# Mirror transposes spread one to a half block pair, and even batches' logits half a pair later

## The chip, the cores and the metric

The kernel runs on one core of one Trainium2 chip. The metric is device time in microseconds (us) of one launch; lower is better. The engines are PE (TensorE), DVE (VectorE), ACT (ScalarE), POOL (GpSimd) and SP (SyncE, which here only issues DMAs). Each engine takes its own instructions in the order in which they were written.

## The reference, cut to what matters

Attention without a softmax, gated by `u`, then a mixture of experts over every token. Eight sequences of 2816 tokens, width 256, query width 64:

```python
scores = (1 / S) * z @ z.T              # one z for queries and keys: scores are symmetric
attn   = np.maximum(scores, 0.0) ** 2
x      = (u * (attn @ v)).reshape(N, D) # N = 22528, D = 256

y      = relu(x @ w1_dense) @ w2_dense
e      = argmax(x @ w_gate, axis=1)     # 8 experts
y     += gate * relu(x @ w1[e]) @ w2[e] # one expert for each token, gate = its softmax weight
```

## The kernel before, in words

**Blocks, pairs, groups.** Each sequence (here called an attention batch) is 22 blocks of 128 tokens. `av` (line 525) works on a pair of blocks: in two passes `p` over the 22 key blocks `x` it adds up `attn @ v` for both in one pair of PSUM banks, 88 small matmuls (line 552). Between the passes and at the end `tick` runs, once for each block. Pairs belong to groups: each attention batch has a group of two blocks and then five of four, 48 groups in all. A group's relu-squared scores lie in a tile `A`, of which three buffers exist (line 74), so group n+3 is written where group n lay. The tile framework makes the first write into a reused buffer wait for all readers of its former content, DMAs included.

**Scores and their mirror.** `scores` (line 368) puts products of `z` into a PSUM pair; `relu` (line 390) has ACT or DVE copy them out (lines 398, 400) and then ACT, DVE or POOL square them into `A` (lines 411, 413). Since scores are symmetric, a group n need not compute those key blocks that are the rows of group n-2: `far_steps` (line 436) yields up to four steps, each of which issues one DMA transpose from the tile of group a = n-2 into the tile of group n (line 446) on SP's queue. Steps wait in the list `turning`, are put there when group a's first pair begins, and are taken from it within `av` at fixed `x` (line 559), if the planner holds their source ready.

**The planner.** The order on PE, ACT, DVE and SP is fixed at build time. Python code keeps a clock `now`, which each matmul advances, and a time at which each engine comes free; `offer` and `run` hand work to the engine that is free first, `fill` puts the scores of later groups between the matmuls of `av`, and `key_at` says from when a key block of a group may be read. In its first pass over a group `av` reads the key blocks in the order of `key_at` (line 543). None of these times is enforced on the chip: there an instruction waits only for its place in its queue and for its data.

**Gate and transposed rows.** When a pair is done, `gate_x` (line 575) has DVE multiply it by `u` into `pays` and SP transpose it into `xT` (line 581); SP also loads `ut`, the rows of `u`, two pairs ahead into three buffers (line 146).

**Routing.** Blocks are routed in batches `q` of 11 (line 42), unaligned with the pairs. `routing(q)` is queued at a tick, and at the next `fill` with a free PSUM pair `logits` (line 599) multiplies the batch's 11 `xT` blocks by `w_gate` (line 607). DVE and ACT then find each token's expert and place, and POOL scatters the rows to the experts' regions in DRAM. Since 11 is odd, a batch with even q ends on the first block of a pair and a batch with odd q on the second. After attention the experts' part runs from the scattered rows.

Of the kernel before, what the change touches and what calls it, by code (L numbers as in the profile page):

```python
# [19 lines left out]
def kernel(  # L20
# [23 lines left out]
    starts = [sum(sizes[:q]) for q in range(len(sizes) + 1)]  # L44
# [39 lines left out]
    def banks(x, name, shape=(P, 2, 4 * P), dt=F32):  # L84

        return ps.tile(list(shape), dt, name=name, tag=f"b{x}")
# [46 lines left out]
    now = [0.0]  # L133
# [7 lines left out]
    def load_u(g, gate=False):  # L141
        ut = aw.tile([P, 2, D], F32, name="ut", bufs=3)
        if gate:
            nc.vector.memset(ut[:, 0, 0:1], 0.0)
        b, i = divmod(g, nK)
        nc.sync.dma_start(out=ut[:], in_=uf[:, b, i:i + 2, :])
        ut_of[g] = ut[:]
# [134 lines left out]
    def offer(ready, rank, ways, then=None):  # L282
        count[0] += 1
        todo.append((rank, count[0], ready, ways, then))
# [44 lines left out]
    def until(cond):  # L329

        while cond() is None:
            pick = best()
            assert pick is not None
            now[0] = max(now[0], pick[0][0])
            give(pick)
        now[0] = max(now[0], cond())
        run(now[0])

    def pe(t):
        now[0] += t  # L340
        run(now[0])


    left, far, key_at = {}, {}, {}
# [7 lines left out]
    def open_group(n):  # L352
        if n not in A:
            A[n] = aA.tile([P, nK, 4 * P], BF, name="A", tag="A")
# [6 lines left out]
    def take_pair():  # L361
        return pairs.pop(0)[1]

    def give_pair(t, x):
        pairs.append((t, x))
        pairs.sort()
# [64 lines left out]
    def can_turn(n, m):  # L431
        _, i0, w = groups[n]
        ts = [key_at.get((m, k)) for k in range(i0, i0 + w)]
        return None if None in ts else max(ts)

    def far_steps(a):

        n = a + 2
        if n >= len(groups) or far[n] != [a]:
            return []  # L440
        (b, i0, w), (_, j0, wj) = groups[n], groups[a]

        def step(i):
            assert n - 1 in A
            open_group(n)
            nc.sync.dma_start_transpose(out=A[n][:, j0:j0 + wj, i * P:(i + 1) * P],
                                        in_=A[a][:, i0 + i, :wj * P])
            if i == w - 1:
                for j in range(wj):
                    key_at[n, j0 + j] = now[0] + 10.0  # L450

        return [(a, lambda i=i: step(i)) for i in range(w)]

# [2 lines left out]
    def fill(n, force=False):  # L456

        if jobs and jobs[0][0] <= now[0] and room(1):
            jobs.pop(0)[1]()
            return True  # L460
        m = ahead(n)
        busy = sum(1 for op in todo if op[0] in (1, 4))
        if m is not None and room(1) and busy <= (4 if n < 2 else 2):
            scores(m, left[m].pop(0))
            return True
        return False
# [7 lines left out]
    def v_at(n, k):  # L474

        return 3.3 + 2.6 * (4 * k // nK) if n == 0 else 0.0

    def need(n, k):

        while max(key_at.get((n, k), 9e9), v_at(n, k)) > now[0]:  # L480
            if fill(n):
                continue
            pick = best()
            ts = [t for t, _ in pairs if t > now[0]]
            ts += [max(key_at[n, k], v_at(n, k))] if (n, k) in key_at else []
            assert pick is not None or ts
            if pick is not None and (not ts or pick[0][0] <= min(ts)):
                now[0] = max(now[0], pick[0][0])
                give(pick)
            else:  # L490
                now[0] = min(ts)
        run(now[0])

    turning = []
# [8 lines left out]
    def swap_rows(n):  # L503

        keep[0] = 0
        if ahead(n) is None:
            until(lambda: pairs[0][0] if pairs else None)
            x = take_pair()
            touch(x)
            touch(x)  # L510
            give_pair(now[0] + 0.1, x)
            return
        until(lambda: pairs[1][0] if len(pairs) > 1 else None)
        x = take_pair()
        touch(x)
        m = ahead(n)
        scores(m, left[m].pop(0))
        m = ahead(n)
        if m is None:
            touch(x)  # L520
            give_pair(now[0] + 0.1, x)
        else:
            scores(m, left[m].pop(0), x)

    def av(n, i, between):
        b, i0, w = groups[n]
        if i == i0:
            turning.extend(far_steps(n))
        keep[0] = 0
        if n == 0 and i == i0:  # L530

            fill(n)
            need(n, 0)
        until(lambda: pairs[0][0] if pairs else None)
        ox = take_pair()
        o = banks(ox, "o")
        for p in range(2):
            rest = list(range(nK))
            for x in range(nK):
                k = rest[0]  # L540
                if i == i0 and p == 0:

                    k = min(rest, key=lambda k: (max(key_at.get((n, k), 9e9), v_at(n, k)), k))
                    need(n, k)
                rest.remove(k)
                if n == 0 and i == i0 and p == 0 and x in (12, 14, 16):
                    load_u(2 * (x - 12) // 2, gate=True)
                for h in range(2):
                    r = slice(h * dq, (h + 1) * dq)
                    j = p ^ h  # L550
                    c = (i + j - i0) * P
                    nc.tensor.matmul(out=o[:, j, 0:D], lhsT=A[n][r, k, c:c + P],  # L552
                                     rhs=v_of[b][r, k, :], start=(p == 0 and x == 0),
                                     stop=(p == 1 and x == nK - 1))
                pe(0.1092)
                keep[0] = 2 - p if x >= nK - 12 else 0
                if x % 2 == 1 and x < nK - 1:
                    fill(n)
                if x % 7 == 3 and turning:
                    t = can_turn(turning[0][0] + 2, turning[0][0])  # L560
                    if t is not None and t <= now[0] and turning[0][0] + 1 in A:
                        turning.pop(0)[1]()
            if p == 0:
                swap_rows(n)
                between()

        def done(t):
            give_pair(t + 0.1, ox)

        g = b * nK + i  # L570
        offer(now[0] + 0.2, 0, {"dve": (0.63, lambda eng: gate_x(g, o))}, done)
        keep[0] = 0


    def gate_x(g, o):
        g0 = g % (2 * G)
        x = pays[:, g0:g0 + 2, 0:D]
        assert g + 1 < 2 * G or (g - 2 * G in placed and g + 1 - 2 * G in placed)
        nc.vector.tensor_mul(x, o[:, :, 0:D], ut_of.pop(g))  # L579
        xT = aw.tile([P, 5, P], BF, name="xT", bufs=8)  # L580
        nc.sync.dma_start_transpose(
            out=xT[:], in_=pays[:, g0:g0 + 2, :].rearrange("p n r -> p (n r)")[:, 0:5 * P])
        for j in range(2):
            xT_of[g + j] = xT[:, 3 * j:3 * j + 2, :]
# [397 lines left out]
    def at(tick, fn):  # L982
        later.setdefault(tick, []).append(fn)
# [10 lines left out]
    for b in range(B):  # L994
        t = b * nK
# [38 lines left out]
    def routing(q):  # L1034
        def first():
            bank_of[q] = take_pair()
            logits(q)
            now[0] += 0.6
            offer(now[0] + 0.2, 0, {"dve": (1.3, lambda eng: route_a(q))}, middle)

        def middle(t):
            give_pair(t, bank_of[q])
            jobs.append((t + 2.5, second))

        def second():
            bank_of[q] = take_pair()
            route_pre(q)
            now[0] += 0.25
            chain(now[0] + 0.2, route_b(q), last)

        def last(t):
            give_pair(t, bank_of[q])
            routed.append(q)
            waiting.extend(range(starts[q], starts[q + 1]))

        jobs.append((now[0], first))
# [11 lines left out]
    LAG = 5  # L1068
    for q in range(nQ - 2):
        t = starts[q + 1] - 1 + LAG  # L1070
        at(t, lambda q=q: routing(q))
    for n, q in enumerate((nQ - 2, nQ - 1)):
        at(nB + 2 * n, lambda q=q: late_routing(q))
        at(nB + 2 * n + 1, lambda q=q: late_places(q))
# [36 lines left out]
    for s in range(NT - MAYBE + 2):  # L1111
# [4 lines left out]
        if s % 3 == 1 and waiting:  # L1116
# [5 lines left out]
    n = nc.values_load(used[0:1, 0:1], min_val=0, max_val=NH,  # L1122
                       skip_runtime_bounds_check_because="made by the table")
# [34 lines left out]
```

## Time and profile before

| | us |
|---|---|
| median of 3 runs | 885.77 (883.65 to 889.91) |
| the profiled execution | 887.47 |
| its span, first to last instruction | 885.8 |
| PE busy | 864.5 |
| ACT busy | 738.6 |
| DVE busy | 701.2 |
| POOL busy | 485.2 |
| mirror transposes issued (`A<-A`) | 128 |
| `xT` transposes issued | 88 |

Durations come from the profiled execution. Busy time is the time in which an engine has an instruction of its own at work; issuing a DMA and waiting are not counted. A timeline row gives start, duration, engine, source line, operation, the tile written and read, the count, and in brackets the idle time of the engine before it with what ended that. `SPq` rows are the DMA issues of SP's queue: their duration is that of the issue, and the data lands later. Attention takes about the first 560 us, the experts' part the rest.

### The profile page before, as it was taken

Reading aid. Unit: us, or ns where it says so; the run is one execution under the profiler, and the core shown is the slowest. Engines: PE = TensorE matmul, PEld = TensorE weight load, DVE = VectorE, ACT = ScalarE, POOL = GpSimd, SP = SyncE. Lnnn points to the kernel's source line nnn. Section 1 sums busy time; section 2 is a strip of 40 time slices with the busy share of each in tenths; the row PEclk is TensorE's granted clock in tenths of the full one; section 3 lists DMA queues with packets and bytes.
Section 4 is the critical chain, followed back from the end, with each engine's and each line's share of the span. In section 5 each row is a group of like instructions: output and inputs, shape, how many; then the busy total and the mean of one; then the engine's idle time right before and its main releaser. Section 6 shows DMA issues by size and latency. Waiting matters only on the chain.

```text
span 885.8 us, 30592 instructions
## 1 busy us (share of the span) xinstructions
PE 864.5 (98%) x12257; PEld 759.7 (86%) x12257; DVE 701.2 (79%) x1320; ACT 738.6 (83%) x913; POOL 485.2 (55%) x532
## 2 busy tenths in 40 slices
PE   8999999999998999999999999999999999999996
PEld 5788888898886888888888888888888888889996
DVE  7999999998996999999998997656665445546664
ACT  7999998998996998998998997477777777777774
POOL 8203343434533534434434544488888888887665
PEclk9999999999999999999999999999999999999998
DMA  6795997998898899899899896555565555544333
GB/s 148 148 174 117 146 185 145 172 174 170 153 165 168 154 181 190 127 197 198 131 196 172 151 159 112 103 133 128 129 132 122 117 120 121 123 113 110 97 100 82
DMA packets 257871, 127.64 MB, mean 144 GB/s; under 512 B 225470, under 2 KB 232894, under 8 KB 257728
## 3 DMA queue, kind: packets, MB, share of 16 engines
q1 hardware_dynamic: 230112, 70.24, 47.6%
q0 software_dynamic: 27616, 55.44, 29.2%
q8 instruction: 96, 1.57, 0.8%
q14 instruction: 47, 0.39, 0.2%
HBM read 61.54 MB, written 37.16 MB: 111 GB/s over the span
## 4 chain that ended last, share of the span: by engine, by line
PE 73%; DVE 7%; issue 6%; POOL 6%; DMA 4%; ACT 3%; SPq 0%; POOLq 0%; DVEq 0%; ACTq 0%
PE o L552 37%; PE h_ps L909 14%; PE yy L917 13%; PE s L383 8%; POOL out_dram L935 5%; DMA xT<-pays 3%; DVE r L400 2%; DVE A L413 2%; ACT A L411 1%; POOL A L413 1%; PE lg L607 1%; ACT r L398 1%; DVE pays L579 1%; DMA out_dram<-ring,ix 1%; DVE zn L113 1%
## 5 line engine op out<-in xcount | busy, mean ns | idle before, releaser
L552 PE MATMUL o<-vb,A 64*128 64x256 bf16 x7744 | 493.7, 270 | 2.6 <-POOL A L413 1.8
L552 PEld LDWEIGHTS <-A 64*128 64x128 bf16 x7744 | 408.1, 94 | 53.9 <-POOL A L413 3.0
L697 POOL DMA_INDIRECT xs<-pays,pi x176 | 196.9, 1119 | 271.1 <-DVE pi L695 207.1
L398 ACT ACTIVATE r<-s 128x1024 f32<-128x1024 f32 x274 | 270.0, 1011 | 26.1 <-PE s L383 22.1
L411 ACT ACTIVATE A<-r 128x1024 bf16<-128x1024 f32 (+1 forms) x257 | 261.3, 1042 | 5.3 <-DMA A<-A 2.7
L912 ACT ACTIVATE ring<-h_ps 128x1024 bf16<-128x1024 f32 x180 | 183.9, 1023 | 89.2 <-PE h_ps L909 87.3
L413 DVE TENSOR_TENSOR A<-r 128x1024 bf16<-128x1024 f32 x167 | 201.8, 1221 | 5.8 <-DMA A<-A 4.0
L400 DVE TENSOR_SCALAR r<-s 128x1024 f32<-128x1024 f32 (+1 forms) x158 | 190.5, 1214 | 4.3 <-POOL A L413 1.8
L933 DVE SCALAR_TENSOR_TENSOR ring<-yy,me,ring 128x256 f32<-128x256 f32 x180 | 86.8, 482 | 123.0 <-ACT ring L932 86.3
L935 POOL DMA_INDIRECT out_dram<-ring,me x140 | 146.4, 1046 | 39.8 <-issue 23.5
L383 PE MATMUL s<-zT 64*128 64x512 bf16 (+1 forms) x944 | 157.9, 359 | 1.6 <-ACT zT L192 0.6
L917 PEld LDWEIGHTS <-ring 128*128 128x128 bf16 x1440 | 140.0, 98 | 16.2 <-issue 0.3
L917 PE MATMUL yy<-w2d,ring 128*128 128x256 bf16 x720 | 108.0, 273 | 0.1
L917 PE MATMUL yy<-ring 128*128 128x256 bf16 x720 | 108.0, 273 | 0.0
L909 PE MATMUL h_ps<-ring,w1d 128*128 128x256 bf16 x720 | 93.3, 273 | 0.8 <-DVE pays L579 0.8
L909 PE MATMUL h_ps<-ring 128*128 128x256 bf16 (+1 forms) x880 | 93.7, 253 | 0.0
L897 DVE COPY ring<-wall 128x2048 bf16 x110 | 80.7, 748 | 8.6 <-DVE ring L933 4.2
L909 PEld LDWEIGHTS <-ring 128*128 128x128 bf16 x880 | 74.3, 98 | 6.8
L909 PEld LDWEIGHTS <-w1d 128*128 128x128 bf16 x720 | 70.1, 98 | 9.0 <-issue 1.0
L579 DVE TENSOR_TENSOR pays<-o,ut 128x512 bf16<-128x512 f32 x88 | 60.3, 685 | 17.6 <-PE o L552 17.1
L383 PEld LDWEIGHTS <-zT 64*128 64x128 bf16 x944 | 58.0, 94 | 16.0 <-issue 3.4
L932 ACT COPY ring<-yy 128x256 f32<-128x256 f32 x180 | 66.1, 367 | 1.8 <-PE yy L917 1.8
(120 smaller groups left out, 358.0 us busy)
## 6 DMA issues: line engine op xcount, KB each, us to landing
ut<-in_u_dram SPq DMA_DIRECT2D x88, 256.0 KB
vb<-in_v_dram POOLq DMA_DIRECT2D x16, 384.0 KB
vb<-in_v_dram POOLq DMA_DIRECT2D x16, 320.0 KB
wall<-in_moe_w_dram POOLq DMA_DIRECT2D x16, 256.0 KB
xs<-pays,pi POOLq DMA_INDIRECT x176
zr<-in_z_dram POOLq DMA_DIRECT2D x7, 352.0 KB
out_dram<-ring,me POOLq DMA_INDIRECT x140
A<-A SPq DMA_TRANSPOSE x128
```

The costliest lines, as they stand in the source:

```text
L383: nc.tensor.matmul(out=s[:, h, y * c:(y + 1) * c], lhsT=zT[r, k + h, :], rhs=zT[r, i0:i0 + w, :], start=True, stop=True)
L398: nc.scalar.activation(r[:, :, :c], s[:, :, :c], AF.Relu, scale=1.0 / S)
L400: nc.vector.tensor_scalar(out=r[:, :, :c], in0=s[:, :, :c], scalar1=1.0 / S, scalar2=0.0, op0=ALU.mult, op1=ALU.max)
L411: nc.scalar.activation(a, r, AF.Square)
L413: (nc.gpsimd if eng == "pool" else nc.vector).tensor_mul(a, r, r)
L552: nc.tensor.matmul(out=o[:, j, 0:D], lhsT=A[n][r, k, c:c + P], rhs=v_of[b][r, k, :], start=(p == 0 and x == 0), stop=(p == 1 and x == nK - 1))
L697: ins = nc.gpsimd.indirect_dma_start(out=xs, out_offset=bass.IndirectOffsetOnAxis(ap=pi[:], axis=0), in_=pays[:, g % (2 * G), 0:ROW].bitca ...
L909: nc.tensor.matmul(out=h_ps[:, f, hs, :], lhsT=w1(c, f), rhs=xT[:, hs, c, :], start=(c == 0), stop=(c == 1))
L912: nc.scalar.activation(h, h_ps[:].rearrange("p f h t -> p f (h t)"), AF.Relu)
L917: nc.tensor.matmul(out=y[:, k, :], lhsT=h[:, f, j * P:(j + 1) * P], rhs=w2(f), start=(f == 0), stop=(f == 3))
L933: nc.vector.scalar_tensor_tensor(out=ys, in0=y[:, 1, :], scalar=me[:, j, 0:1], in1=yd, op0=ALU.mult, op1=ALU.add)
L935: ins = nc.gpsimd.indirect_dma_start(out=out, out_offset=bass.IndirectOffsetOnAxis(ap=ids[j], axis=0), in_=ys, in_offset=None, bounds_chec ...
```

## The change

Two edits, and a number that goes with the first:

- a mirror step is taken at `x == 3` of the first pass and at `x == 10` of the second, where it was taken at x = 3, 10 and 17 of both. So a pair hands out two steps, one in each half, where it handed out a group's four one after the other;
- the key blocks that a group gets by mirror are held readable 6 planner units after the last step, where it was 10;
- the logits of a batch with even q are queued one tick later (`starts[q + 1]` is odd there), in the middle of a pair instead of at its end; those with odd q stay.

```diff
             if i == w - 1:
                 for j in range(wj):
-                    key_at[n, j0 + j] = now[0] + 10.0
+                    key_at[n, j0 + j] = now[0] + 6.0
...
                 if x % 2 == 1 and x < nK - 1:
                     fill(n)
-                if x % 7 == 3 and turning:
+                if x == (3, 10)[p] and turning:
                     t = can_turn(turning[0][0] + 2, turning[0][0])
                     if t is not None and t <= now[0] and turning[0][0] + 1 in A:
                         turning.pop(0)[1]()
...
     LAG = 5
     for q in range(nQ - 2):
         t = starts[q + 1] - 1 + LAG
-        at(t, lambda q=q: routing(q))
+        at(t + starts[q + 1] % 2, lambda q=q: routing(q))
```

## The prediction

> **What bounds the kernel now.** I read the page's engine table first, then the attention stage alone, then what TensorE waited for.
>
> ```profile
> PE 864.5 (98%) x12257; PEld 759.7 (86%) x12257; DVE 701.2 (79%) x1320; ACT 738.6 (83%) x913; POOL 485.2 (55%) x532
> ...
> 10.30:562.90 552.60, 542.16 (x9130) 470.77 (x9130) 511.29 (x914) 499.91 (x544) 227.58 (x225) 0.99 0.94 160
> 562.90:885.80 322.90, 315.62 (x3060) 284.38 (x3059) 182.98 (x395) 231.93 (x362) 249.66 (x288) 0.99 0.50 116
> ```
>
> The second and third rows are stretches: length, then busy time of PE, PEld, DVE, ACT, POOL, the granted clock and the DMA share. Both edits lie in the first stretch, attention. TensorE is busy 542.2 of 552.6 us there, so no more than some 10 us can be won; but DVE (511.3) and ACT (499.9) are nearly as full, and the DMA engines have a share of 0.94. A stall of DVE or ACT thus finds little slack to go into.
>
> ```profile
> PE lg L607 <- DMA xT<-pays: 6.6, 4, 4.2
> PE o L552 <- POOL A L413: 1.8, 2, 0.9
> ...
> DVE A L413 <- DMA A<-A: 4.0, 2, 3.2
> ...
> ACT A L411 <- DMA A<-A: 2.7, 1, 2.7
> ```
>
> In the table of waits (total us, times, longest) TensorE's largest is the logits' wait for the transposed rows xT, 6.6 us in four places. The two rows below decide what I forecast: squares on DVE and ACT that write a score buffer A sometimes wait for a mirror transpose that still reads the buffer's former content. So far that costs 6.7 us.
>
> ```profile
> 128.67 5.24 DMA xT<-pays
> 195.11 6.75 DMA xT<-pays
> 266.14 7.33 DMA xT<-pays
> 470.88 7.60 DMA xT<-pays
> ```
>
> The chain of waits holds the four late xT transfers: issue time, and time from issue to landing. All four belong to even batches. The worst, on the timeline:
>
> ```profile
> 257.36 0.68 DVE L579 TENSOR_TENSOR pays<-o,ut 128x512 bf16<-128x512 f32 x1
> 258.29 7.18 SPq L446 DMA_TRANSPOSE A<-A  x4
> 265.57 0.53 SPq L146 DMA_DIRECT2D ut<-in_u_dram  x1
> 266.14 1.21 SPq L581 DMA_TRANSPOSE xT<-pays  x1
> 270.33 1.06 ACT L411 ACTIVATE A<-r 128x1024 bf16<-128x1024 f32 x1 [2.69 <-DMA A<-A]
> 270.37 1.22 DVE L413 TENSOR_TENSOR A<-r 128x1024 bf16<-128x1024 f32 x1 [3.22 <-DMA A<-A]
> 271.51 0.68 DVE L579 TENSOR_TENSOR pays<-o,ut 128x512 bf16<-128x512 f32 x1
> 273.52 0.20 PE L607 MATMUL lg<-wg,xT 128*128 128x8 bf16 x2 [4.19 <-DMA xT<-pays]
> ```
>
> Two things happen. The gate of 257.36 has its xT issued only at 266.14, since four mirror transposes stand ahead in SP's queue, and TensorE idles 4.19 us. And the last of the four, issued before 265.47, lands at 270.3; the first squares into the buffer that it reads hold both ACT and DVE till then, and DVE's next gate waits behind.
>
> **Part 1: the logits' wait goes.** With xT no longer behind four transposes, and even batches read half a block pair later (2.4 us of matmuls plus scores), the 6.6 us should go: the gate's xT now has at most one mirror transpose ahead of it, and two and a half pairs of about 6 us until it is read. Less than 6.6 is gone only if something else is late at that point; that is part 2. The stall has an aftermath:
>
> ```profile
> 268.40:280.80 12.40, 8.12 (x125) 6.16 (x122) 6.16 (x15) 5.25 (x7) 3.34 (x3) 0.86 0.90 176
> 470.00:485.00 15.00, 13.63 (x249) 11.98 (x245) 11.83 (x25) 10.73 (x14) 6.42 (x7) 1.00 1.11 187
> ```
>
> After the 4.19 us idle time the granted clock is 0.86 over 12.4 us, (1 - 0.86) x 12.4 = 1.7 us lost; after the shorter wait near 478 it stays 1.00. So part 1 is worth 6.6 + 1.7 = 8.3 us.
>
> **Part 2: the reuse of A comes due.** There are three A buffers, so group n+3 writes where group n lay. Before, all four transposes that read group n are handed out within its first block pair, and the last is issued well ahead of the first square into the buffer (265.47 against about 267 above, which was too late; 334.47 against 340.59 in the rows below, which was not): hence only three waits in all. Now a group's fourth transpose is handed out at the second slot of a later pair. In the built order of instructions SP then holds, for each block pair: ut, transpose, xT, transpose. The planner's slots tie SP to nothing; what paces this row is that ut and xT wait for the gate of the pair before. I time it on the place where one batch ends and the next begins, with rows of before:
>
> ```profile
> 329.33 5.14 SPq L446 DMA_TRANSPOSE A<-A  x4
> ...
> 336.34 0.68 DVE L579 TENSOR_TENSOR pays<-o,ut 128x512 bf16<-128x512 f32 x1
> ...
> 337.21 0.52 SPq L146 DMA_DIRECT2D ut<-in_u_dram  x1
> 337.78 1.21 SPq L581 DMA_TRANSPOSE xT<-pays  x1
> ...
> 339.07 1.93 ACT L398 ACTIVATE r<-s 128x1024 f32<-128x1024 f32 x2
> ...
> 340.59 1.22 DVE L413 TENSOR_TENSOR A<-r 128x1024 bf16<-128x1024 f32 x1
> ...
> 340.87 1.06 ACT L411 ACTIVATE A<-r 128x1024 bf16<-128x1024 f32 x1
> ...
> 341.88 0.69 DVE L579 TENSOR_TENSOR pays<-o,ut 128x512 bf16<-128x512 f32 x1
> ```
>
> Gate 336.34, ut 337.21. From 337.78 the changed queue has one transpose (5.14 / 4 = 1.29), xT (1.21 and 0.06 between), so the second transpose issues at 340.35. The same sequence stands once in the trace of before, at the start of a batch, and gives the same: gate at 152.59, second transpose 4.66 later where the first took 2.13:
>
> ```profile
> 152.59 0.68 DVE L579 TENSOR_TENSOR pays<-o,ut 128x512 bf16<-128x512 f32 x1
> ...
> 153.74 2.13 SPq L446 DMA_TRANSPOSE A<-A  x1
> 155.92 1.27 SPq L581 DMA_TRANSPOSE xT<-pays  x1
> 157.25 2.52 SPq L446 DMA_TRANSPOSE A<-A  x2
> ```
>
> The first squares into the reused buffer are due at 340.59 on DVE and 340.87 on ACT. **How long from issue to landing** is the unknown. It can't be under the issue itself, 1.2 us; the four late xT took 5.24 to 7.60. Those four are picked for being late, so I take a bit less than the lowest, 4.6 us, an estimate; bounds 1.2 and 7.6. Landing is then at 344.95, and both engines stand still about 4.2 us.
>
> What TensorE feels is read from who is queued behind. On ACT the held square has two relus behind it, the second of which frees the PSUM pair into which the moved logits go.
>
> ```profile
> L398 ACT ACTIVATE r<-s 128x1024 f32<-128x1024 f32 x268 | 266.5, 1020 | 25.4 <-PE s L383 21.5 <-POOL A L413 1.0 <-DVE A L413 0.6
> L411 ACT ACTIVATE A<-r 128x1024 bf16<-128x1024 f32 x251 | 257.9, 1052 | 5.3 <-DMA A<-A 2.7 <-DVE r L400 1.3 <-DVE vb L128 0.8
> ...
> 548.80 4.82 PE o L552 x88
> ```
>
> ACT is through at 344.95 + 1.05 + 2 x 1.02 = 348.0. TensorE, whose next pair starts with the gate of 341.88, reaches the logits after 44 matmuls of 54.8 ns and some scores, at about 344.6. It waits 3.4 us. On DVE the gate behind its square is done by 344.95 + 1.22 + 0.69, sooner, so ACT sets the price.
>
> There are four such handovers in each of eight attention batches (the last batch's last goes to no attention group), about seven full rounds. For the other three I put the same landing (8.6 us after the gate, 9.4 after the pair's start) against the place in the built order at which TensorE first needs work behind the held square:
> - into a batch's last group: the relu chain ends 3.1 after the landing, TensorE is there 10.7 after the pair's start: 1.8 us.
> - into the fourth group: relu 2.1 after the landing against 10.9: 0.6 us.
> - into the fifth: 2.1 against 12.3: nothing.
>
> Sum for a batch 3.4 + 1.8 + 0.6 = 5.8, times 7 = 41 us. Each us of latency more or less is worth about three a batch, 20 in all. At about 2.4 us only the first place is left, 1.2 a batch, and part 2 is no more than part 1's 8.3.
>
> **The rest, at nothing.** The same 128 transposes are issued; mirrored rows are read at the earliest one pair and a half after they are handed out, 9 us, and last in the first pass (the new key), so TensorE's own wait for them is covered up to a latency of about 6; beyond, it is below 1 us a group. Scatters of even batches come 3 us later; a slot of pays is still rewritten over 8 us (150 matmuls in the built order) after its scatter, and that margin is the cover.
>
> **A rule on the clock.** The Trainium skill, page "TensorE: Matmul & The Clock Gate", section "Part 1: The HAM clock gate (the "warmup" mystery)", says that after one idle window of about 3.4 us TensorE falls to half clock until it was busy for such a window. The trace agrees with its two waits, 4.19 us followed by 0.86 and the shorter one by 1.00. By that rule a stall of 3.4 us stands on the edge, and if each of the seven fell over it, seven times 1.7 would add 12 us; That is in no term of the sum.
>
> **Sum.** 887.47 (profiled execution; span 885.8) - 8.3 + 41 = 920. That execution lies 1.7 above the median of the runs shown, so 918.5 for the median; measured runs scatter by 883.65 to 889.91, so 1% (8.9 us) is about what can be told from no change.
>
> **Rivals.**
> - Faster: the reuse stays covered. A landing less than 2.4 us after issue, as where queues are empty, leaves 0 to 8 us of part 2 against 8.3: 877.5 (at the bound of 1.2 us) to 885.8. For it: before, only three such waits, and unqueued transfers may be quick. Against: a DMA share of 1.11 in the stretch at 470, and the transpose that ended its issue at 265.47 and took 4.9 us more. Chance 0.08, of it 0.03 faster by over 1%.
> - Much slower: a latency of 6 to 6.5 us, as the share stays over 1 in the batch's second half where v is loaded, and the clock falls at each of the seven longest stalls as it did after the 4.19 us (1.7 each): (1.4 to 1.9) x 20 and 12 more, 955 to 970. Chance 0.15.
> - The spreading doesn't happen: SP, tied to no slot, issues the two transposes back to back ahead of xT. Then the second issues 1.3 us earlier, part 2 shrinks by 7 x 3 x 1.3 = 27, and xT is 1.3 later, which the later logits cover: 891.5. Against it stands the built order, which has xT, and so the wait for its gate, ahead of the second transpose. Chance 0.05.
> - My forecast, 895 to 955: 0.7. The 0.02 that is left is a loss under 1% by the forecast's own mechanism.
>
> The range, 888 to 955, leaves out the fast rival and the worst latencies. Faster by over 1% has 0.03; within 1% 0.05 + 0.05 + 0.02; slower 0.7 + 0.15.
>
> **What would show it.** Right: no TensorE wait for xT at the logits; SP's row alternating ut, A, xT, A; ACT and DVE waits for A<-A grown from 6.7 us to some 50 or more, with the longest where a batch changes; TensorE waiting at logits and scores for ACT relus. Wrong: those waits stay under 10 us, or they grow and TensorE's busy share in attention doesn't fall.

## The result

The changed kernel takes 972.09 us (median; 964.69 to 978.95) against 887.09 (879.69 to 894.82) for the kernel before on the same chip: a ratio of 1.0977, 95% interval 1.0901 to 1.1052. The forecast was 918.5, with 955 as the upper end. So the change is slower, as forecast, but by 85 us and not by 33. (Ratios here leave out executions that ran disturbed as a whole; a median may hold some.)

The profiled execution took 967.89 us. Its engine table, and below it attention and the experts' part as two stretches (length, busy time of PE, PEld, DVE, ACT and POOL, granted clock, DMA share):

```profile
PE 888.9 (92%) x12257; PEld 775.9 (80%) x12257; DVE 700.6 (73%) x1320; ACT 739.6 (77%) x913; POOL 492.7 (51%) x532
```

```profile
10.30:642.30 632.00, 564.78 (x9133) 486.04 (x9128) 510.70 (x913) 502.12 (x546) 233.56 (x225) 0.95 0.81 140
642.30:966.20 323.90, 315.85 (x3066) 284.36 (x3060) 183.96 (x396) 231.93 (x362) 250.93 (x289) 0.99 0.51 116
```

TensorE's busy share falls from 98 to 92%. All of the time lies in attention: 632.0 us for 552.6, while the experts' part stays (323.9 for 322.9). DVE and ACT do the same work as before (510.7 and 502.1 for 511.3 and 499.9); they only stand still more. For TensorE the 79.4 us split into two. Its idle time in attention is 632.00 - 564.78 = 67.2 where it was 10.4: **56.8 us of new waits**. And it is busy 564.8 where it was 542.2, with the same matmuls at a mean clock of 0.95 for 0.99: **22.6 us of slower clock**.

The table of waits (total us, times, longest):

```profile
DVE A L413 <- DMA A<-A: 82.7, 21, 9.6
ACT A L411 <- DMA A<-A: 82.0, 21, 9.6
...
PE s L383 <- DVE pi L695: 25.1, 5, 6.7
...
PE s L383 <- ACT r L398: 15.1, 7, 3.5
PE s L383 <- DVE r L400: 12.7, 4, 8.5
```

The squares' waits for a mirror transpose have grown from 6.7 us to 164.7. TensorE's new waits are for what stands behind a held square on ACT or DVE: the relus that free PSUM. The row with `pi` names a small cast on DVE that stands right behind such a relu (in one of its five places: relu at 220.14, cast at 221.27, TensorE again at 221.41), so it is most likely the same wait. No row of TensorE waiting for xT is left; it was the largest before.

**Where in a batch.** A batch is eleven pairs, counted here from 0. The first squares into a reused buffer fall into pair 2 (into the fourth group), pair 4 (into the fifth), pair 6 (into the last) and pair 8 (batch border: into the next batch's first group). Each row below is the sum line of a view with six stretches: that pair in batches 1 to 6, from its first matmul to the next pair's first. First the kernel before, pairs 2, 4, 6, 8; the first number is the length, the second TensorE's busy time:

```profile
sum 40.15, PE 40.15 PEld 34.30 DVE 39.32 ACT 39.35 POOL 15.98; mean PE 6.69 PEld 5.72 DVE 6.55 ACT 6.56 POOL 2.66
...
sum 35.61, PE 35.61 PEld 30.55 DVE 34.51 ACT 35.15 POOL 10.78; mean PE 5.93 PEld 5.09 DVE 5.75 ACT 5.86 POOL 1.80
...
sum 34.53, PE 34.53 PEld 31.67 DVE 34.18 ACT 34.24 POOL 13.39; mean PE 5.75 PEld 5.28 DVE 5.70 ACT 5.71 POOL 2.23
...
sum 47.75, PE 40.70 PEld 32.84 DVE 32.59 ACT 28.12 POOL 19.57; mean PE 6.78 PEld 5.47 DVE 5.43 ACT 4.69 POOL 3.26
```

And the changed kernel, in the same order:

```profile
sum 52.79, PE 42.83 PEld 35.84 DVE 34.32 ACT 37.42 POOL 12.81; mean PE 7.14 PEld 5.97 DVE 5.72 ACT 6.24 POOL 2.14
...
sum 34.67, PE 34.67 PEld 31.18 DVE 33.77 ACT 34.67 POOL 11.58; mean PE 5.78 PEld 5.20 DVE 5.63 ACT 5.78 POOL 1.93
...
sum 78.76, PE 43.38 PEld 35.45 DVE 36.34 ACT 37.20 POOL 19.76; mean PE 7.23 PEld 5.91 DVE 6.06 ACT 6.20 POOL 3.29
...
sum 55.41, PE 43.16 PEld 36.47 DVE 33.87 ACT 30.03 POOL 19.26; mean PE 7.19 PEld 6.08 DVE 5.64 ACT 5.01 POOL 3.21
```

Idle time of TensorE is length minus busy: it was 0, 0, 0 and 7.1 us, it is 10.0, 0, 35.4 and 12.3. So 35.4 of these 57.7 us arise at one place, into a batch's last group, at which the prediction had put 1.8 a batch. The worst of the six, on the timeline:

```profile
366.09 3.31 SPq L116 DMA_TRANSPOSE zT<-zn  x2
...
368.73 0.68 DVE L579 TENSOR_TENSOR pays<-o,ut 128x512 bf16<-128x512 f32 x1
...
370.96 1.33 SPq L146 DMA_DIRECT2D ut<-in_u_dram  x1
...
373.63 1.28 SPq L581 DMA_TRANSPOSE xT<-pays  x1
373.85 0.59 POOL L129 DMA_DIRECT2D vb<-in_v_dram  x1
...
374.95 1.30 SPq L446 DMA_TRANSPOSE A<-A  x1
...
384.34 2.00 ACT L411 ACTIVATE A<-r 128x1024 bf16<-128x1024 f32 x2 [9.61 <-DMA A<-A]
...
386.77 0.61 PE L383 MATMUL s<-zT 64*128 64x512 bf16 x2 [8.52 <-DVE r L400]
```

The gate is at 368.73. The prediction had the second transpose of a pair at 4.0 us after the gate and its landing 4.6 later. Here two transposes of the next batch's `zT` (line 116) stand in the queue, ut is issued 2.2 us after the gate instead of 0.9, and the transpose 6.2 after it, with a load of v (`vb`) issued in between; and then it takes 9.4 us until the squares go on, and TensorE has idled for 8.52. At the border of the same batch there is no zT, and both numbers are near the prediction's 4.0 and 4.6 (3.8 and 5.3):

```profile
390.11 0.68 DVE L579 TENSOR_TENSOR pays<-o,ut 128x512 bf16<-128x512 f32 x1
...
393.91 1.27 SPq L446 DMA_TRANSPOSE A<-A  x1
...
399.19 1.06 ACT L411 ACTIVATE A<-r 128x1024 bf16<-128x1024 f32 x1 [4.82 <-DMA A<-A]
```

The place shown is the worst. The same two times, read from the trace in all six batches and averaged:

| place | gate to issue of the fourth transpose | issue to the first held square | together |
|---|---|---|---|
| predicted, everywhere | 4.0 | 4.6 | 8.6 |
| into the fourth group | 3.7 | 6.4 (5.5 to 7.4) | 10.1 |
| into the last group | 6.4 | 6.9 (5.6 to 9.4) | 13.2 |
| batch border | 3.9 | 4.5 (3.2 to 5.5) | 8.3 |

### The profile page after: what moved, and what is told of

It is laid out like the page before. It is cut to its first block, busy times and chain, and to the rows that moved or that the text cites. A ratio compares the mean times of both kernels' runs of the same rounds, so it can differ in the third digit from the quotient of the medians.

```text
span 966.2 us, 30573 instructions
## 1 busy us (share of the span) xinstructions
PE 888.9 (92%) x12257; PEld 775.9 (80%) x12257; DVE 700.6 (73%) x1320; ACT 739.6 (77%) x913; POOL 492.7 (51%) x532
## 4 chain that ended last, share of the span: by engine, by line
PE 47%; DMA 13%; DVE 12%; issue 10%; ACT 5%; POOL 5%; SPq 5%; POOLq 0%; DVEq 0%; ACTq 0%
PE o L552 17%; PE h_ps L909 12%; PE yy L917 12%; DMA A<-A 12%; DVE r L400 5%; POOL out_dram L935 4%; PE s L383 4%; ACT r L398 4%; DVE A L413 3%; SPq L581 2%; SPq L446 2%; ACT A L411 2%; DVE pays L579 2%; DVE zn L113 1%; DMA out_dram<-ring,ix 1%
## 5 line engine op out<-in xcount | busy, mean ns | idle before, releaser
L552 PE MATMUL o<-vb,A 64*128 64x256 bf16 x7744 | 510.6, 276 | 2.4 <-ACT A L411 0.9
L552 PEld LDWEIGHTS <-A 64*128 64x128 bf16 x7744 | 422.7, 97 | 57.0 <-issue 5.9
L697 POOL DMA_INDIRECT xs<-pays,pi x176 | 203.0, 1154 | 333.1 <-DVE pi L695 269.9
L411 ACT ACTIVATE A<-r 128x1024 bf16<-128x1024 f32 (+1 forms) x252 | 256.8, 1043 | 82.3 <-DMA A<-A 82.0
L398 ACT ACTIVATE r<-s 128x1024 f32<-128x1024 f32 (+1 forms) x279 | 274.2, 1013 | 26.4 <-PE s L383 23.7
L413 DVE TENSOR_TENSOR A<-r 128x1024 bf16<-128x1024 f32 x172 | 208.0, 1223 | 90.6 <-DMA A<-A 82.7
L383 PE MATMUL s<-zT 64*128 64x512 bf16 (+1 forms) x944 | 163.7, 371 | 53.2 <-DVE pi L695 25.1
L400 DVE TENSOR_SCALAR r<-s 128x1024 f32<-128x1024 f32 (+1 forms) x153 | 184.0, 1210 | 6.9 <-PE s L383 4.5
L383 PEld LDWEIGHTS <-zT 64*128 64x128 bf16 x944 | 61.3, 96 | 81.7 <-issue 68.1
```

The source lines that it names most:

```text
L383: nc.tensor.matmul(out=s[:, h, y * c:(y + 1) * c], lhsT=zT[r, k + h, :], rhs=zT[r, i0:i0 + w, :], start=True, stop=True)
L398: nc.scalar.activation(r[:, :, :c], s[:, :, :c], AF.Relu, scale=1.0 / S)
L400: nc.vector.tensor_scalar(out=r[:, :, :c], in0=s[:, :, :c], scalar1=1.0 / S, scalar2=0.0, op0=ALU.mult, op1=ALU.max)
L411: nc.scalar.activation(a, r, AF.Square)
L413: (nc.gpsimd if eng == "pool" else nc.vector).tensor_mul(a, r, r)
L697: ins = nc.gpsimd.indirect_dma_start(out=xs, out_offset=bass.IndirectOffsetOnAxis(ap=pi[:], axis=0), in_=pays[:, g % (2 * G), 0:ROW].bitca ...
```

## The experiments

After the result the theory was: the loss is the reuse of A by transposes that land late, and it is larger than predicted because into the last group the fourth transpose is late, by zT ahead of it in SP's queue, by v's loads beside it, or by both. The rivals: the moved logits take part; the spreading costs by itself, whenever the last transpose lands; the clock or the DMA engines are worse throughout.

### Only the logits moved

On the kernel before:

```diff
-        at(t, lambda q=q: routing(q))
+        at(t + starts[q + 1] % 2, lambda q=q: routing(q))
```

> Only the later logits of even batches; the transposes stay four in a row. My theory: the four waits for xT (6.6 us) shrink to under 2 us and no idle time is long enough to drop the clock, so 6 to 8 us faster than the kernel before: about 880 us against 887. Rival, that moving the logits is itself a cost (scatters later, PSUM pair taken at a worse point): 887 or more.

Measured: 885.24 us against 889.22, a ratio of 0.995 (0.990 to 0.9999). The waits:

```profile
DVE A L413 <- DMA A<-A: 7.1, 2, 5.5
...
ACT A L411 <- DMA A<-A: 5.6, 1, 5.6
...
PE lg L607 <- DMA xT<-pays: 2.8, 2, 2.5
```

Moving the logits helps by about half a per cent, some 4 us, less than the 6 to 8 expected, though the interval (0.1 to 9 us) does not exclude them: with four transposes still ahead of xT, 2.8 of the 6.6 us of waiting stay, and the squares' waits are 12.7 for 6.7.

### Only the transposes spread

The changed kernel with the logits' line put back:

```diff
-        at(t + starts[q + 1] % 2, lambda q=q: routing(q))
+        at(t, lambda q=q: routing(q))
```

> Only the spread transposes with their 6 units; the logits stay where they were. My theory, that the reuse of the three A buffers makes nearly all of the loss: 960 to 980 us, the waits of squares for A<-A at 150 us or more, as with both edits. Rival, that the moved logits standing behind the held relu make the loss where a batch changes: some 25 to 35 us less than with both edits, 940 to 945.

Measured: 972.05 us, a ratio of 1.0965 (1.0873 to 1.1056), the same as the whole change. The squares' waits are 139.2 us, a little under the 150 expected. The spreading makes all of the loss; in the total the moved logits neither add to it nor give anything back. Where in a batch the loss lies does shift: TensorE's idle time in pairs 2, 4, 6 and 8 is 12.9, 11.4, 24.2 and 9.8 us here, 58.3 in all.

### A fourth buffer

The changed kernel with four A buffers. To make room, only two experts' weights are kept and used in turn, so that the routed half of the output is another one:

```diff
-    aA = pool("aA", 3)
+    aA = pool("aA", 4)
...
-    wall = const.tile([P, E, WD], BF, name="wall")
+    wall = const.tile([P, E // 4, WD], BF, name="wall")
```

> Both edits, with four A buffers in place of three, so that a square never meets a transpose that still reads. The space comes from the expert weights: only two experts' worth is held, and the experts' part reads weights at other offsets, with the same sizes and counts, so the routed half of the output is not the reference's. My theory: the waits of squares for A<-A fall to about nothing, the clock stays up, and the time is 875 to 885 us. Rival, that transposes spread between other transfers are slow in themselves, so that TensorE or SP waits for them whatever the buffers: 930 us or more.

Measured: 894.63 us (878.09 to 906.13) against 889.22, a ratio of 0.9962 (0.9889 to 1.0034). The median lies above the 875 to 885 expected, but far from the rival's 930. The waits:

```profile
DVE A L413 <- DMA A<-A: 8.7, 3, 4.4
...
ACT A L411 <- DMA A<-A: 7.3, 3, 4.0
```

With the reuse one group further away the squares' waits fall from 164.7 to 16.0 us, and the loss is gone, with the spreading, the new key and the moved logits all still there. That settles the cause: it is the reuse of the buffer. Spread transposes cost nothing by themselves that this ratio could tell.

### zT one pair earlier

In the changed kernel zT's transposes queued two ticks sooner:

```diff
-            soon(t + 6, lambda b=b: turn_z(b + 1, 0, nK // 2), 0.4)
-            soon(t + 7, lambda b=b: turn_z(b + 1, nK // 2, nK), 0.4)
+            soon(t + 4, lambda b=b: turn_z(b + 1, 0, nK // 2), 0.4)
+            soon(t + 5, lambda b=b: turn_z(b + 1, nK // 2, nK), 0.4)
```

> Both edits, with the two zT transposes of the next attention batch queued two ticks earlier, so that they no longer stand ahead of the transposes that the last group's buffer waits for. My theory, that they made the waits into the last group (6 to 8 us a batch) long: these fall to some 2 to 3 us, the other places stay, 930 to 950 us. Rival, that the loads of v on POOL's queue in that half of the batch make those transposes land late: the waits into the last group stay over 5 us and the time at 965 to 975.

Measured: 978.32 us, a ratio of 1.1046 (1.0943 to 1.1149) where the whole change has 1.0977: no gain, and above the rival's 965 to 975 too. The sums for pairs 4, 6 and 8 say why:

```profile
sum 56.14, PE 40.26 PEld 33.32 DVE 37.30 ACT 33.73 POOL 15.73; mean PE 6.71 PEld 5.55 DVE 6.22 ACT 5.62 POOL 2.62
...
sum 50.60, PE 38.52 PEld 33.20 DVE 32.19 ACT 34.78 POOL 15.91; mean PE 6.42 PEld 5.53 DVE 5.37 ACT 5.80 POOL 2.65
...
sum 68.54, PE 49.89 PEld 39.35 DVE 34.68 ACT 31.42 POOL 25.91; mean PE 8.32 PEld 6.56 DVE 5.78 ACT 5.24 POOL 4.32
```

Idle time into the last group falls from 35.4 to 12.1 us, as it should if zT delays that place. But into the fifth group, where there was none, it is 15.9, and at the border 18.7 for 12.3. The hold moves to other places, and no less is lost in all. (The copies on DVE that make `zn` move along with zT, and with them part of the order that the planner gives ACT and DVE; the next experiment moves zT alone.)

### zT behind the fourth transpose

The other direction, by the order of SP's queue alone: zT is issued at the end of pair 5, after the fourth transpose of that place; no other engine's order changes.

```diff
-        nc.sync.dma_start_transpose(
+        at(b * nK - 11, lambda: nc.sync.dma_start_transpose(
```

> The changed kernel with the two zT transposes, 3.3 us of SP's queue, issued behind the fourth mirror transpose of a batch's last group instead of ahead of it; nothing else moves on any engine. Theory (into the last group the hold is long because zT delays the fourth transpose's issue from about 4 to about 8 us after its gate): the fourth issues some 4 us after its gate again, the hold there falls from 4.3 to 9.6 us to about 3, and since the next place has one more pair to make up for the 3.3 us, it grows by no more than 1.5: TensorE gets back some 3 us and part of the clock in each of six batches, 940 to 955 us. Rival 1 (the queue makes the loss good at the next place, as when zT was moved ahead): the batch border takes it all, 967 to 980 us. Rival 2 (the long landing, up to 9.3 us, is what counts there, not the issue): the hold stays above 5 us, above 960 us.

Measured: 965.75 us, a ratio of 1.0927 (1.0854 to 1.0999), a little under rival 1's 967 to 980. Pairs 6 and 8:

```profile
sum 46.22, PE 38.17 PEld 32.62 DVE 30.87 ACT 31.82 POOL 16.72; mean PE 6.36 PEld 5.44 DVE 5.14 ACT 5.30 POOL 2.79
...
sum 74.87, PE 48.34 PEld 38.46 DVE 34.57 ACT 31.43 POOL 23.55; mean PE 8.06 PEld 6.41 DVE 5.76 ACT 5.24 POOL 3.93
```

Into the last group idle time falls to 8.1 us, and at the border it rises from 12.3 to 26.5. Rival 1 holds: the next place pays. In four of the six batches the fourth transpose of the border issues 6.8 to 8.0 us after its gate, where it was 3.8 to 3.9, and the square follows its issue about as soon as before (4.4 to 5.5 us). Over the four places idle time falls from 57.7 to 43.4 us, and the time by 6 us, within the two intervals. The expectation that one more pair makes up for the 3.3 us failed; SP's queue has no such slack, as its rows show there:

```profile
373.42 6.23 SPq L116 DMA_TRANSPOSE zT<-zn  x2
...
380.32 2.38 SPq L581 DMA_TRANSPOSE xT<-pays  x1
```

Here the issue of the two zT alone takes 6.23 us instead of 3.31, and that of an xT 2.38 instead of 1.2: what an issue takes isn't a constant.

### Without the loads of v

The changed kernel without the loads of v after the first batch (all batches use the first one's v, so the output is another one):

```diff
-                soon(t + 10 + 2 * h, lambda b=b, h=h: load_v(b + 1, h, 4))
+                soon(t + 10 + 2 * h, lambda b=b, h=h: v_of.__setitem__(b + 1, v_of[0]))
```

> The changed kernel without the loads of v after the first attention batch: all batches multiply with the first one's v, so the output is another one, and the 1.4 MB of loads in each batch's second half are gone, with their 28 small memsets on DVE. The order on PE, ACT and SP stays. Theory (into the last group and at the batch border the fourth transpose lands 5.5 to 9.3 us after its issue, and zT's issue takes longer, because v's loads share the DMA engines): the latencies there fall to about 4, the holds of the squares into the last group from 4.3 to 9.6 us to 3 to 5, the squares' waits for A<-A from 165 us to about 100, and with the clock 945 to 955 us. Rival (the latency comes from the transposes among themselves): the waits stay above 140 us, above 962 us.

Measured: 949.81 us, a ratio of 1.0778 (1.0697 to 1.0859), as the theory has it; the squares' waits fall to 116.7 us, less far than to the 100 expected, but well under the rival's 140. First the sum for pair 6, then the two stretches (attention and the experts' part):

```profile
sum 56.39, PE 39.36 PEld 33.30 DVE 31.89 ACT 33.64 POOL 16.73; mean PE 6.56 PEld 5.55 DVE 5.31 ACT 5.61 POOL 2.79
```

```profile
10.40:613.57 603.17, 559.54 (x9131) 482.82 (x9128) 509.55 (x885) 500.99 (x545) 220.91 (x197) 0.97 0.72 130
613.57:945.50 331.93, 315.63 (x3062) 284.33 (x3060) 182.89 (x396) 231.96 (x362) 247.35 (x289) 0.98 0.49 113
```

And the place of the timeline above, in this kernel:

```profile
349.92 3.45 SPq L116 DMA_TRANSPOSE zT<-zn  x2
...
351.50 0.68 DVE L579 TENSOR_TENSOR pays<-o,ut 128x512 bf16<-128x512 f32 x1
...
358.30 1.27 SPq L446 DMA_TRANSPOSE A<-A  x1
...
362.75 2.00 ACT L411 ACTIVATE A<-r 128x1024 bf16<-128x1024 f32 x2 [5.10 <-DMA A<-A]
```

zT's issue is as long as before (3.45), and the fourth transpose as late after its gate (6.8 us, 6.2 with the loads). But the squares go on 4.45 us after it, not 9.4. So it is in all six batches: from issue to square 2.6 to 4.5 us, 3.4 in the mean, where it was 5.6 to 9.4 and 6.9. Into the fourth group, before v's loads begin, it hardly changes (6.0 for 6.4). Idle time into the last group is 17.0 us instead of 35.4, and attention 603.2 instead of 632.0, 29 us less with v's loads away. How much of that the kernel before would gain as well was not run; it has 10.4 us of idle time in attention. (The experts' part is 8 us longer with TensorE as busy as before; other tokens are routed there, and why that is slower is not shown.)

The Trainium skill, page "DMA: Bandwidth & Descriptors", section "SWDGE vs HWDGE vs iDMA", says that transfers issued from GpSimd and those from SyncE run on the same DMA engines, though their descriptors are made in different places. The runs are in line with it: v's loads are issued on POOL's queue, SP's transposes on another, and taking away the one brings the other's landing at this place from 9.4 to 4.45 us.

### Three transposes to a pair

A dose between before and after: three slots a pair, where the change has two and the kernel before six. Only SP's order changes.

```diff
-                if x == (3, 10)[p] and turning:
+                if x in ((3, 10), (3,))[p] and turning:
```

> The changed kernel with a third slot, x = 10 of the first pass, so that a pair hands out three transposes; nothing but SP's order moves. In that order the fourth transpose of a group stands right behind ut or xT of the second pair, 1.7 to 3 us after its gate instead of 4 to 8. Theory (the time goes by when the fourth transpose issues): the squares' waits for A<-A fall from 165 us to below 40, only the batch border is left with about 1 us of loss, 885 to 900 us. Rival (transposes that lie between the other transfers cost by themselves, whenever the last one issues): above 930 us.

Measured: 913.84 us, a ratio of 1.0247 (1.018 to 1.0315): between theory and rival. From the profiled execution (917.27 us), the squares' waits and the sum for pair 8:

```profile
DVE A L413 <- DMA A<-A: 40.5, 9, 12.8
...
ACT A L411 <- DMA A<-A: 36.2, 8, 9.7
```

```profile
sum 74.66, PE 45.24 PEld 37.36 DVE 34.65 ACT 31.42 POOL 20.45; mean PE 7.54 PEld 6.23 DVE 5.78 ACT 5.24 POOL 3.41
```

By the ratios, 9.8% and 2.5%, three quarters of the loss go with one slot more. The squares' waits fall to 76.7 us, not below 40. In pairs 2, 4 and 6 of the six batches TensorE now idles no more than 0.2 us in all, so the theory holds there; what is left is the border alone, with 29.4 us of idle time (7.1 before) and 45.2 busy (40.7 before), where the theory had 1 us a batch.

### Three to a pair, without the loads of v

The two edits above together:

> The kernel with three transposes to a pair, again without the loads of v after the first batch. There only the batch border is left, where the fourth transpose lands 6.8 to 11.9 us after its issue. Theory (v's loads): these latencies fall to 4 or 5 us, the squares' waits from 77 us to below 25, 885 to 893 us. Rival (the transposes among themselves, zT's above all): the waits stay above 60 us, 905 to 915 us.

Measured: 897.43 us, a ratio of 1.02 (1.012 to 1.028). The waits and the two stretches:

```profile
DVE A L413 <- DMA A<-A: 12.6, 5, 4.6
...
ACT A L411 <- DMA A<-A: 8.6, 4, 4.6
```

```profile
10.10:562.92 552.82, 541.82 (x9129) 472.72 (x9130) 508.89 (x884) 502.14 (x544) 226.06 (x197) 0.99 0.78 142
562.92:894.80 331.88, 315.62 (x3060) 284.31 (x3060) 181.96 (x396) 231.92 (x362) 249.27 (x289) 0.98 0.48 113
```

The waits fall from 76.7 to 21.2 us, as the theory had it, and attention takes 552.8 us, as much as before. The total lies above the forecast 885 to 893 only for the experts' part, 331.9 us here and in the other run without v's loads, 322.9 before. So the border's remaining loss with three to a pair is drawn out by v's loads too: its idle time falls from 29.4 to 6.9 us.

### Four to a pair, behind the gate

From these runs: keep four in a row, so that all are issued in a group's first pair, but behind xT instead of ahead of it. The kernel before with the moved logits and

```diff
-                if x % 7 == 3 and turning:
+                if (x in (10, 17) if p == 0 else x in (3, 10)) and turning:
```

> The kernel before with two edits: the logits of even batches one tick later, as in the change, and the mirror steps taken at x = 10 and 17 of the first pass and x = 3 and 10 of the second, so that a pair still hands out four transposes, but behind ut and xT in SP's queue instead of ahead of xT. Theory (what costs is only a fourth transpose that issues in the second of two pairs): the fourth issues about 1.6 + 4 x 1.3 = 6.8 us after a gate, in the first of the two pairs, so the squares' waits for A<-A stay near the 13 us of the moved logits alone, xT has nothing ahead of it and TensorE no wait for it: 880 to 886 us. Rival (any other order of SP's queue turns up as a new wait elsewhere): 887 to 900 us.

Measured: 879.62 us, a ratio of 0.9937 (0.9908 to 0.9965): 0.6% faster than the kernel before, and a little under the 880 to 886 expected. The squares' waits for transposes, expected near 13 us, are gone but for this one, and attention in the profiled execution has 3.7 us of idle time and a clock of 1.00:

```profile
DVE A L413 <- DMA A<-A: 1.0, 1, 1.0
```

```profile
10.65:552.47 541.82, 538.09 (x9131) 470.51 (x9129) 510.88 (x913) 503.19 (x545) 238.30 (x225) 1.00 0.93 163
```

Attention is 10.8 us shorter there than in the profile of before, 6.7 of it idle time and 4.1 TensorE's busy time; by the medians (884.69 before) the gain is 5.1 us. From the moved logits alone (a ratio of 0.995, 0.990 to 0.9999) it can't be told apart in time, only in the waits: 1.0 us for 12.7 on the squares, and none for xT where 2.8 were left.

## Why the prediction was wrong in size

**Bound and part 1: right, with probably too much gain.** TensorE had 10 us to win in attention. The waits for xT are gone after the change. That they are worth 8.3 us can't be seen there. Moving the logits alone gives 4.0 us (0.1 to 9 by its interval), and with the transposes behind xT it is 5.1 (3 to 8), so the term was probably nearly twice too large.

**Part 2, the mechanism: right.** The queue alternates ut, A, xT, A, but for places where two transposes of A stand together; the squares' waits grow from 6.7 to 164.7 us; TensorE waits behind the held relus. The fourth buffer shows that this is the whole loss, as far as its ratio can tell.

**Part 2, the sum: the first step that failed.** It was 3.4 at the border, 1.8 into the last group, 0.6 into the fourth, nothing into the fifth. TensorE's idle time a batch, from the sums of six, is 2.0, 5.9, 1.7 and 0. The border, which was timed on rows, came out smaller; the fifth is right; **the term "into a batch's last group" measures 5.9 us instead of 1.8**, and the one into the fourth group 1.7 instead of 0.6. The three others were put at the border's landing, "8.6 after the gate, 9.4 after the pair's start", as if the queue were the same at all four. It isn't: the zT transposes stand in it ahead of the last group's fourth transpose, in the kernel before too, and that transpose's landing falls beside v's loads. In the mean of six batches it is 2.4 us late in issue and 2.3 in landing, 13.2 us after its gate instead of 8.6; on the place shown, the worst, 15.6. The first part alone can be moved to another place but hardly away (zT earlier, zT later); without v's loads the second part is gone (3.4 us, under the 4.6). Into the fourth group the issue is on time and the landing takes 6.4 instead of 4.6, with or without v's loads; why is open. The sum of 41 us stands against 56.8 + 6.6 = 63.4 (the new idle time, and what made good for the waits that left).

**The clock at nothing: the second step that failed.** Part 1 took 1.7 us of clock as a gain, and the 12 us of the rule stood "in no term of the sum". Attention lost 22.6 us to it. The prediction priced a drop at 1.7 and expected one at most for each of seven border stalls; but the stalls into the last group are the long ones, and in all six batches the clock is down there (0.79 to 0.93), besides three of the six borders and two of the six places into the fourth group. Together: 63.4 - 41 = 22.4 and 22.6 + 1.7 = 24.3 make 46.7 of the 47.7 us by which the profiled execution (967.89) missed the 920.2 forecast for it; the last 1.0 is in the experts' part.

**The rival "much slower"** came nearest, 955 to 970 with a clock that falls at long stalls, and got 0.15; the median, 972.09, lies just above it. Its latency of 6 to 6.5 us is close to the mean of the three places (6.4, 6.9 and 4.5), but it put the longest stalls at the border, and there the latency was the short one; part of the agreement is luck. "Faster" and "the spreading doesn't happen" are out; by the run with a fourth buffer, nothing of the loss is tied to transposes being spread as such.

**The rest at nothing: borne out.** With four buffers the new key, the mirrored rows and the later scatters are all in place, and the time is that of before.

What stays open: why, with v's loads running, the landing is 9.4 us in one batch and not in every one; why it takes over 6 us into the fourth group without them; and how much of the border's loss with three to a pair is zT's own, whose issue is drawn out there as well.

## What to carry to other kernels

Before a transfer is moved to a later place in its queue, write down for every buffer that it reads who overwrites it next, and time each such handover on its own: what else stands in the queue and which loads run beside it differ from place to place, and the worst place, not the one that is easiest to time, carries the sum. A stall that idles TensorE for microseconds also costs clock; here that was two fifths of what the waits cost. A hand-out in a row was not the fault of the kernel before: with the same four in a row behind xT instead of ahead of it, TensorE's waits for xT and the squares' waits are both gone.

## What the hardware showed that was not expected

**The clock falls after stalls far under 3.4 us, and not after every one.** Two pairs of the changed kernel, from the views summed above, and below them three stretches of 3.41 us out of these pairs:

```profile
345.23:354.90 9.67, 8.05 (x124) 6.50 (x120) 5.98 (x14) 7.11 (x9) 2.56 (x3) 0.84 0.79 144
...
431.05:440.29 9.24, 6.65 (x124) 5.69 (x121) 5.47 (x12) 5.69 (x8) 1.93 (x2) 1.00 1.06 146
```

```profile
348.49:351.90 3.41, 1.85 (x43) 1.41 (x39) 1.92 (x3) 1.96 (x2) 0.35 (x1) 1.00 0.85 206
351.90:355.31 3.41, 3.35 (x30) 2.58 (x31) 2.10 (x9) 3.08 (x5) 1.65 (x3) 0.50 0.29 65
...
437.23:440.64 3.41, 1.88 (x32) 1.75 (x33) 3.27 (x10) 3.38 (x5) 0.97 (x1) 1.00 0.57 132
```

In the first pair TensorE is idle 9.67 - 8.05 = 1.6 us, and the clock is 0.84; in the second 2.6 us, and it stays 1.00. The Trainium skill's rule that the prediction cites (one idle window of some 3.4 us) does not give the first, if the whole window must be idle. The record of the clock in the trace shows more: in attention it is either full or half, and each of the thirteen stretches at half clock, 61.4 us in all, is 3.41 us long or twice that and begins on one grid of 3.41 us. Cut along this grid, the profiles of all eleven kernels have 1775 stretches of attention at full clock. All 48 in which TensorE idled for 60% or more were followed by half clock, none below 35% was, and in between 21 of 58 were. The rows above lie there: 1.56 us of idle time was followed by half clock, 1.53 wasn't. So a stall of 2.6 us that falls across an edge of the grid can pass, and one of 1.6 us within a stretch can cost 1.7 us of clock.

The Trainium skill, page "TensorE: Matmul & The Clock Gate", section "Part 1: The HAM clock gate (the "warmup" mystery)", also says that the window runs free of the kernel. The trace agrees: the stretches keep to their grid wherever the stalls lie.

**The issue of a DMA transpose and its landing depend on what else is moved.** One and the same pair of zT transposes took SP 3.31 us in one order and 6.23 in another; a transpose of A landed 4.45 us after its issue without v's loads and 9.4 with them, at the same place of the same batch.
